# A token mixer and its MLP on one core: a written order for the opening, two attention pieces per chunk, and 512-token blocks in the second row

## The chip, the cores and the metric

The kernel runs on one core of one Trainium2 chip. The metric is the device time in microseconds (us), as the median of several runs. The core's engines work side by side, each through its own list of instructions in order, and wait for one another by semaphores: TensorE (PE in the profile; its weight loads are PEld), VectorE (DVE), ScalarE (ACT), GpSimd (POOL) and SyncE (SP, which here only issues transfers). Within the core TensorE multiplies from SBUF into eight banks of PSUM.

## The reference

Two parts. The first is a linear attention with a decay per channel, over 4 sequences (B) of 768 tokens, 8 heads of 48 channels; the second is a gated MLP over its 3072 output rows.

```python
for t in range(S):                       # S = 768
    cur = einsum('bhd,bhe->bhde', u[None] * kt, vt)
    y[:, :, t] = einsum('bhd,bhde->bhe', rt, state + cur)
    state = wt[:, :, :, None] * state + einsum('bhd,bhe->bhde', kt, vt)

x = y.transpose(0, 2, 1, 3).reshape(B * S, H * D)      # 3072 x 384
gate = 1.0 / (1.0 + exp(-(x @ w_gate)))                # 384 x 1536
val = x @ w_val
out = (gate * val) @ w_out                             # 1536 x 384
```

All of it is float32. Each MLP product is made of three products of a rounded high part (`hi`) and the rest (`lo`), in the type fp32r: lo times hi, hi times lo, hi times hi.

## The kernel before, in words

**Chunks and rows.** A sequence is cut into 6 chunks of 128 tokens. The four chunks with the same place in the four sequences make a *row*: n = 0 to 5, 512 tokens each. Chunk q is sequence q % 4 of row q // 4, and there are 24. Attention turns a chunk into 128 rows of x, and the MLP works on a row, or on half of one, in 12 slices f of 128 hidden units.

**The opening** is rows 0 and 1 (chunks 0 to 7 enter the MLP, chunks 8 to 11 are prepared). In it the 12 weight slices also come from memory for the first time and are unpacked, each by five instructions on VectorE and ScalarE. After it (row 2 on) a fixed loop takes over: a row of 512 tokens and one slice after another, with the attention of the next row's chunks spread among them, and a second look at the weights for bounds. That loop is not touched.

**Pieces.** The opening is built of small named pieces; the names below are used in the prediction, with a number for the chunk q or the slice f.

- For a chunk: `pin`, `tok` (loads on SP), `b1_` `b2_` `b4_` (three products on GpSimd), `b3_` (a sum on VectorE), `pk` and `pr` (a scan and a product each, on VectorE, lines 370 to 392), `guard` (ScalarE, line 397), `fade` (VectorE), `tk` (transposes on TensorE), `kT` (copy on ScalarE), `sm` (sums: 32 small matmuls, line 466), `mid` and `keep` (the state at mid-chunk and at the end), `sc` (scores: 32 matmuls of line 419 and 16 or 32 of line 429), `m0` `m1` (masks on VectorE, line 451), `mx` (mix: 64 small matmuls, line 490), `y0` `y1` (VectorE, line 497), `tx` (transposes of the result), `xh` and `xl` (high part on ScalarE, rest on VectorE, line 515).
- For a slice of weights: `words` (load, line 274), `wg` (ScalarE, line 281), `wb` and `wt` (VectorE, lines 286 and 290), `wh` (ScalarE, line 313), `wl` (VectorE, line 316).
- For an MLP block of group g and slice f: `pg` and `pu` (nine matmuls each, line 523), `sg` (sigmoid, ScalarE), `hm` (product, VectorE, line 541), `hh` (ScalarE, line 545), `hl` (VectorE, line 549), `dn` (down product, line 558: three matmuls of 384 columns per chunk).

**Groups.** Before, a group is two chunks, so 256 tokens: rows 0 and 1 have two groups each, and every `pg` and `pu` of the opening has 256 columns. From row 2 on they have 512, and the down product is turned (line 576).

**What sets the order.** `Plan` is a planner that runs while the program is built: each piece has an engine, a cost, what it comes after, a rank, and the buffers it takes and gives. `TURNS` ranks chunks and weight slices against each other, `COMES` orders the loads, `LAGS` ranks the groups, `ROOM` counts buffers. The planner emits a piece when its engine would be free, which gives every engine its list.

**Buffers.** Two each of `pin`, `tok`, `bon` and x; a load into one waits until its last reader is done. PSUM has one bank for `pg`, one for `pu`, four for the down sums and two for all attention pieces (`att_bank`). In the opening `sg`, `hh` and `hl` come from a pool named `early` with four buffers each; it is closed for a pool named `late` with two when the opening ends.

Of the kernel before, what the change touches and what calls it, by code (L numbers as in the profile page):

```python
# [169 lines left out]


class Plan:


    def __init__(self, room):
        self.ops, self.room = {}, dict(room)

    def add(self, name, engine, cost, after, rank, work=None, take=(), give=()):
        self.ops[name] = (engine, cost, [a for a in after if a], rank, work, take, give)

    def run(self):
        left = {n: set(o[2]) for n, o in self.ops.items()}
        room, free, ends, order, started = self.room, {}, [(0.0, "")], [], set()
        transfers = [n for n in sorted(self.ops, key=lambda n: self.ops[n][3]) if self.ops[n][0] == "SP"]
        while ends:
            now = min(ends)[0]
            for e in [e for e in ends if e[0] <= now]:
                ends.remove(e)
                if e[1] in self.ops:
                    for r in self.ops[e[1]][6]:  # L190
                        room[r] += 1
                    for n in left:
                        left[n].discard(e[1])
            moved = True
            while moved:
                moved = False
                for n in sorted((n for n in self.ops if n not in started and not left[n]), key=lambda n: self.ops[n][3]):
                    engine, cost, _, _, work, take, _ = self.ops[n]
                    if engine and free.get(engine, 0.0) > now or engine == "SP" and n != transfers[0]:
                        continue  # L200
                    if any(room[r] < take.count(r) for r in take):
                        continue
                    for r in take:
                        room[r] -= 1
                    if engine:
                        free[engine] = now + cost
                        ends.append((now + cost, "-" + n))
                    if engine == "SP":
                        transfers.pop(0)
                    ends.append((now + cost + (2.0 if engine == "SP" else 0.13 if engine else 0.0), n))  # L210
                    started.add(n)
                    order.append(n)
                    if work:
                        work()
                    moved = True
                    break
        assert len(started) == len(self.ops), sorted(set(self.ops) - started)
        return order
# [3 lines left out]
def tile_kernel(ctx: ExitStack, tc: tile.TileContext, dec: bass.AP, tok: bass.AP, wts: bass.AP, u: bass.AP, out: bass.AP):  # L222
# [388 lines left out]

    plan = Plan(ROOM)
    rank = {n: i for i, n in enumerate(TURNS.split())}
    comes = {n: i for i, n in enumerate(COMES.split())}

    def add(name, engine, cost, after, rank, f=None, *args, take=(), give=()):
        plan.add(name, engine, cost, after, rank, f and (lambda: f(*args)), take, give)

    add("ub", "SP", 1.4, [], comes["ub"], lambda: nc.sync.dma_start(ub, u.partition_broadcast(P)))
    for q in range(3 * B + 2):  # L620
        k = rank.get(f"c{q}", 99)
        add(f"pin{q}", "SP", 2.9, [], comes[f"p{q}"], load_pin, q, take=["pin"])
        add(f"tok{q}", "SP", 2.3 + 1.4 * (not q), [], comes[f"t{q}"], load_tok, q, take=["tok"])
        if q > 3 * B:
            continue
        add(f"b1_{q}", "POOL", 1.35, [f"tok{q}", "ub"], k, bonus1, q, take=["bon"])
        add(f"b2_{q}", "POOL", 1.15, [f"b1_{q}"], k, bonus2, q)
        add(f"b3_{q}", "DVE", 0.57, [f"b2_{q}"], k + 0.3, bonus3, q)
        add(f"b4_{q}", "POOL", 1.45, [f"b3_{q}"], k, bonus4, q)
        add(f"pk{q}", "DVE", 2.2, [f"pin{q}"], k, prep_k, q, take=["eg"])  # L630
        old = q >= B
        if old:
            add(f"fade{q}", "DVE", 0.38, [f"pk{q}", f"keep{q - B}"], k + 0.05, fade, q, take=["ready"])
        add(f"pr{q}", "DVE", 2.15, [f"pk{q}"], k + 0.1, prep_r, q)
        add(f"guard{q}", "ACT", 1.26, [f"pr{q}", old and f"fade{q}"], k + 0.5, guard, q, give=["eg"])
        if q == 3 * B:
            continue
        add(f"tk{q}", "PE", 0.4 + 0.5 * (q < 3), [f"pk{q}"], k + 0.1, turn_k, q, take=["bank", "kT"])
        add(f"kT{q}", "ACT", 0.52, [f"tk{q}"], k + 0.1, take_k, q, give=["bank"])
        add(f"sm{q}", "PE", 0.7 + 0.5 * (q < 3), [f"kT{q}", f"tok{q}"], k + 0.15, sums, q, take=["bank", "bank"], give=["kT"])  # L640
        add(f"mid{q}", "DVE" if old else "ACT", 0.36, [f"sm{q}", old and f"fade{q}"], k + 0.12, middle, q, take=["mid"], give=["bank"])
        add(f"keep{q}", "DVE", 0.36, [f"mid{q}"], k + 0.15, keep, q, give=["bank"])
        add(f"sc{q}", "PE", 1.2 + 1.2 * (q < 3), [f"pr{q}", f"mid{q}"], k + 0.2, scores, q, take=["bank", "bank", "at"], give=["pin"] + ["ready"] * old)
        add(f"m0{q}", "DVE", 0.43, [f"sc{q}"], k + 0.2, mask, q, 0)
        add(f"m1{q}", "DVE", 0.43, [f"m0{q}"], k + 0.2, mask, q, 1)
        add(f"mx{q}", "PE", 0.92 + 0.7 * (q < 3), [f"m1{q}"], k + 0.3, mix, q, give=["at"])
        add(f"mid{q}done", None, 0, [f"sc{q}", f"keep{q}"], k, give=["mid"])
        add(f"y0{q}", "DVE", 0.37, [f"mx{q}", f"b4_{q}"], k + 0.3, take_y, q, 0, give=["bank"])
        add(f"y1{q}", "DVE", 0.37, [f"y0{q}"], k + 0.3, take_y, q, 1, give=["bank"])
        first = q % B == 0  # L650
        add(f"tx{q}", "PE", 0.34 + 0.45 * (q < 3), [f"y1{q}", q % B and f"tx{q - 1}"], k + 0.4, turn_x, q, take=["bank"] + ["x"] * first, give=["bon"])
        add(f"xh{q}", "ACT", 0.68, [f"tx{q}"], k, take_x, q)
        add(f"xl{q}", "DVE", 0.58, [f"xh{q}"], k, rest_x, q, give=["bank"])
        add(f"tok{q}done", None, 0, [f"mx{q}", f"sm{q}", f"b4_{q}", q % B and f"tok{q - 1}done"], k, give=["tok"])
    for f in range(NFF):
        k = rank[f"w{f}"]
        add(f"words{f}", "SP", 3.7 + 1.6 * (not f), [], comes[f"w{f}"], fetch, f)
        add(f"wg{f}", "ACT", 1.29, [f"words{f}"], k, w_top, f)
        add(f"wb{f}", "DVE", 0.85, [f"words{f}", f and f"wb{f - 1}"], k, w_body, f, take=["full"])
        add(f"wt{f}", "DVE", 1.39, [f"wb{f}", f"wg{f}"], k, w_join, f)  # L660
        add(f"wh{f}", "ACT", 1.15, [f"wt{f}"], k, w_hi, f)
        add(f"wl{f}", "DVE", 1.42, [f"wh{f}"], k, w_lo, f, give=["full"])
    for g, (n, i0, i1) in enumerate(GROUPS):
        m = i1 - i0
        for f in range(NFF):
            a, name = (n, f, i0, i1), f"{g}_{f}"
            k = 100 + f + LAGS[g]
            soon = k / 1000 - 1
            up_cost = 9 * (0.008 + 0.056 * m)
            need = [f"xl{n * B + i}" for i in range(i0, i1)] + [f"wl{f}", f and f"pu{g}_{f - 1}"]  # L670
            add("pg" + name, "PE", up_cost, need, k, gate, *a, take=["pg", "unit"] + [f"po{i}" for i in range(i0, i1) if f == 0])
            add("sg" + name, "ACT", 0.14 + 0.13 * m, ["pg" + name], soon, sigmoid, *a, give=["pg"])
# [107 lines left out]
```

## Time and profile before

| | |
|---|---|
| time, median of 3 runs | 582.59 us (581.71 to 583.43) |
| the profiled execution, its own time | 581.37 us |
| its span, first to last instruction | 579.6 us |
| PE busy | 551.4 us (95%), 6330 matmuls |
| PEld busy | 476.2 us (82%) |
| DVE busy | 322.8 us (56%) |
| ACT busy | 248.3 us (43%) |
| POOL busy | 100.4 us (17%) |
| granted TensorE clock | 0.999 |

A busy time is the sum over one engine's instructions in the one profiled execution; a share is of the span. In rows of instruction groups the columns are line, engine, operation, what is written and read with its shape, and the count, then busy us and the mean ns of one, then the idle time just before them and what ended it. In rows of the timeline and the chain the first number is the start and the second the duration, in us. In rows of stretches the columns are the stretch, its length, then busy us (and count) of PE, PEld, DVE, ACT and POOL, the granted clock, the DMA share and GB/s. A wait reads "engine, line <- who ended it: us in total, times, longest".

### The profile page before, as it was taken

The page shows a single profiled execution, that of the slowest core. Times are in us where ns is not written, and L with a number is a line of the kernel's source. Part 1 is how long each engine was busy: PE and PEld are TensorE (multiplying, and loading weights), DVE is VectorE, ACT ScalarE, POOL GpSimd, SP SyncE. Part 2 cuts the span into 40 slices and gives each one's busy share as a digit, 9 for nine tenths or more (in the row PEclk, how much of TensorE's full clock was granted, in tenths as well). Part 3 has the DMA queues.
Part 4 walks back from the last instruction along what each step waited for, and adds up shares of the span by engine and source line. Part 5 has one row for each costly group of instructions (what it writes and reads, how often), then busy time and mean ns, then how long its engine had stood idle before and what let it go on. Part 6 is the DMA issues. An engine that isn't in the chain of part 4 may idle for free.

```text
span 579.6 us, 14499 instructions
## 1 busy us (share of the span) xinstructions
PE 551.4 (95%) x6330; PEld 476.2 (82%) x6330; DVE 322.8 (56%) x561; ACT 248.3 (43%) x577; POOL 100.4 (17%) x86
## 2 busy tenths in 40 slices
...
GB/s 283 181 379 366 91 365 2 44 150 95 60 98 58 138 125 1 84 151 119 88 151 101 160 151 77 131 151 55 173 185 34 173 42 43 63 19 1 1 0 58
DMA packets 17203, 67.32 MB, mean 116 GB/s; under 512 B 1904, under 2 KB 3312, under 8 KB 15600
## 3 DMA queue, kind: packets, MB, share of 16 engines
...
q8 instruction: 51, 0.84, 0.6%
q14 instruction: 16, 0.13, 0.1%
...
## 4 chain that ended last, share of the span: by engine, by line
PE 90%; DVE 6%; ACT 1%; DMA 1%; issue 1%; ACTq 0%; SPq 0%; DVEq 0%
PE pu L523 26%; PE pg L523 26%; PE po L576 17%; PE po L558 8%; PE pa L490 3%; PE pa L419 2%; PE pa L429 2%; PE pk L402 2%; PE pv L466 1%; PE px L502 1%; DMA tok<-tok 1%; PE pa L466 1%; DVE w L316 1%; DVE full L290 1%; DVE eg L370 1%
## 5 line engine op out<-in xcount | busy, mean ns | idle before, releaser
L523 PE MATMUL pg<-x,w 128*128 128x256 f32 (+1 forms) x864 | 168.0, 339 | 2.1 <-ACT sg L534 1.5
L523 PE MATMUL pu<-x,w 128*128 128x256 f32 (+1 forms) x864 | 169.8, 341 | 0.0
L523 PEld LDWEIGHTS pg<-x,w 128*128 128x128 f32 x864 | 137.3, 190 | 20.3 <-ACT sg L534 1.9
L523 PEld LDWEIGHTS pu<-x,w 128*128 128x128 f32 x864 | 135.2, 189 | 16.9
L541 DVE TENSOR_TENSOR sg<-pu,sg 128x256 f32<-128x256 f32 (+1 forms) x96 | 53.4, 556 | 120.4 <-PE pu L523 117.7
L545 ACT CAST hh<-sg 128x256 fp32r<-128x256 f32 (+1 forms) x96 | 49.2, 513 | 158.5 <-DVE sg L541 157.9
L534 ACT ACTIVATE sg<-pg 128x256 f32<-128x256 f32 (+1 forms) x96 | 47.0, 489 | 107.1 <-PE pg L523 101.3
L576 PE MATMUL po<-hh,w 128*128 128x512 f32 x288 | 89.2, 391 | 0.0
L363 POOL TENSOR_TENSOR bon<-tok,a 128x384 f32<-128x384 f32 x24 | 37.7, 1573 | 262.4 <-DVE a L359 262.4
L549 DVE TENSOR_TENSOR hl<-sg,hh 128x256 fp32r<-128x256 f32 (+1 forms) x96 | 56.9, 592 | 40.8 <-ACT hh L545 40.6
L576 PEld LDWEIGHTS po<-hh,w 128*128 128x128 f32 x288 | 54.0, 188 | 10.9
L576 PE MATMUL po<-hl,w 128*128 128x512 f32 x144 | 58.3, 405 | 0.0
L352 POOL TENSOR_TENSOR bon<-tok,ub 128x384 f32<-128x384 f32 x24 | 30.9, 1289 | 113.0 <-PE px L502 60.5
L558 PE MATMUL po<-w,hh 128*128 128x384 f32 x192 | 49.0, 336 | 0.0
L497 DVE TENSOR_TENSOR bon<-pa,bon 128x192 f32<-128x192 f32 x48 | 15.2, 351 | 46.8 <-PE pa L490 46.8
L558 PEld LDWEIGHTS po<-w,hh 128*128 128x128 f32 x192 | 34.9, 189 | 0.0
L558 PE MATMUL po<-w,hl 128*128 128x384 f32 x96 | 33.9, 353 | 0.6 <-DVE hl L549 0.6
L370 DVE TENSOR_TENSOR_SCAN eg<-pin,ends 112x516 f32<-112x516 f32 x24 | 30.2, 1257 | 4.1 <-DMA pin<-dec 4.1
L576 PEld LDWEIGHTS po<-hl,w 128*128 128x128 f32 x144 | 27.0, 188 | 5.6 <-DVE hl L549 0.2
L397 ACT ACTIVATE junk<-eg 112x1032 bf16<-112x1032 f32 x24 | 25.6, 1065 | 11.8 <-DVE eg L387 11.8
L387 DVE TENSOR_TENSOR_SCAN eg<-pin,heads 112x516 f32<-112x516 f32 x24 | 30.2, 1256 | 0.0
L355 POOL TENSOR_TENSOR bon<-bon,tok 128x384 f32<-128x384 f32 x24 | 29.6, 1233 | 1.8
...
## 6 DMA issues: line engine op xcount, KB each, us to landing
pin<-dec SPq DMA_DIRECT2D x23, 772.0 KB, 4.7
tok<-tok SPq DMA_DIRECT2D x24, 576.0 KB, 5.5
...
wraw<-wts SPq DMA_DIRECT2D x12, 1151.6 KB, 10.1
...
y<-o ACTq DMA_DIRECT2D x8, 192.0 KB, 1.9
...
```

The costliest lines, as they stand in the source:

```text
L352: nc.gpsimd.tensor_tensor(out=bon[q], in0=tk[q][:, 0:DM], in1=ub, op=ALU.mult)
L355: nc.gpsimd.tensor_tensor(out=bon[q], in0=bon[q], in1=tk[q][:, DM:2 * DM], op=ALU.mult)
L363: nc.gpsimd.tensor_tensor(out=by_head(bon[q]), in0=by_head(tk[q][:, 2 * DM:]), in1=a0, op=ALU.mult)
L370: nc.vector.tensor_tensor_scan(out=e[:, 516:0:-1], data0=t[:, 516:0:-1], data1=ends[:, 516:0:-1], initial=0.0, op0=ALU.mult, op1=ALU.add,)
L387: nc.vector.tensor_tensor_scan(out=e[:, WW:WW + 516], data0=t[:, 0:516], data1=heads[:, 0:516], initial=0.0, op0=ALU.mult, op1=ALU.add,)
L523: nc.tensor.matmul(t, lhsT=w[f][:, cols], rhs=x[n][:, a, k, i0 * C:i1 * C], start=k == 0 and j == 0, stop=k == NKT - 1 and j == 2)
L534: nc.scalar.activation(sg, hid["g", n, f, i0], AF.Sigmoid)
L541: nc.vector.tensor_tensor(out=sg, in0=hid["u", n, f, i0], in1=sg, op=ALU.mult)
L545: nc.scalar.copy(hh, hid["s", n, f, i0])
L549: nc.vector.tensor_tensor(out=hl, in0=hid["s", n, f, i0], in1=hid["hi", n, f, i0].bitcast(F32), op=ALU.subtract)
L558: nc.tensor.matmul(po[n, i][:, :DM], lhsT=h[:, c], rhs=w[f][:, 2 * DM:], start=f == 0 and j == 0, stop=f == NFF - 1 and j == 2,)
L576: nc.tensor.matmul(po[n, k], lhsT=w[f][:, cols], rhs=h, start=f == 0 and j == 0, stop=f == NFF - 1 and j == 2)
```

## The change

Three things, all in the opening.

1. The planner goes. Its place takes a string, `ORDER`, that names every piece in the order in which it is emitted; a table, `todo`, maps each name to its function.
2. `sm`, `sc` and `mx` become two pieces: `ss` (scores_sums: the 32 matmuls of line 419 and the sums, which now write to the free columns of the same two banks) and `sx` (state_mix: the matmuls of line 429 and the mix). Both functions were there already for the loop from row 2 on.
3. Row 1 becomes one group of four chunks, 512 tokens: group 2 is (1, 0, 4), and group 3 is gone. The pools change from `early` to `late` at its first piece, `pg2_0`.

The order itself changes with this. Some differences: on SP `words0` comes ahead of `tok0`, and `tok2` ahead of `tok1`; on ScalarE `wg0` comes first of all; on VectorE the unpacking of slice 0 follows `pr0` at once; the first block, `pg0_0`, comes after `tk2`, before any scores of chunk 2; and row 1 starts when row 0 is through.

```diff
-TURNS = "w10 c0 w6 c2 w1 c3 w0 c8 w3 c4 c1 c9 w7 c11 c7 w2 c6 w8 w11 w4 w5 c5 c12 c10 w9"
-COMES = "p0 t0 p1 ub w0 p2 t1 w1 t2 p3 w2 w3 w6 t3 w5 w4 w11 p4 t4 p5 w9 p6 t7 w7 t5 w10 w8 t6 t8 p7 p11 p8 t9 t11 p12 p9 p10 t10 t12 p13 t13"
-GROUPS = [(0, 0, 2), (0, 2, 4), (1, 0, 2), (1, 2, 4)]
-LAGS = [96.5, 328.5, 417.5, 78.5]
-ROOM = dict(pin=2, tok=2, bon=2, eg=1, ready=2, mid=2, kT=1, at=1, bank=2, x=2, full=1, pg=1, pu=1, unit=4, po0=1, po1=1, po2=1, po3=1)
+GROUPS = [(0, 0, 2), (0, 2, 4), (1, 0, 4)]
+ORDER = """
+pin0 words0 pk0 ub pr0 tk0 tok0 wg0 wb0 kT0 wt0 guard0 wh0 words1 wl0 b1_0 ss0 pin1 b2_0 b3_0 mid0 m00 b4_0 tok2 wg1 keep0 m10 wb1
+sx0 wt1 words2 pk1 wh1 tok1 wl1 pr1 words3 wg2 wb2 y00 b1_1 y10 pin2 tx0 wt2 tk1 xh0 kT1 xl0 b2_1 words4 wh2 ss1 b1_2 b3_1 wl2
+mid1 guard1 b4_1 m01 m11 keep1 b2_2 wg3 sx1 wb3 pk2 pin3 y01 y11 wt3 tx1 tk2 xh1 words5 wh3 xl1 pr2 pg0_0 wg4 pu0_0 kT2 wl3 sg0_0
+tok3 guard2 ss2 hm0_0 wb4 words6 hh0_0 wt4 pg0_1 mid2 pk3 pu0_1 sg0_1 wh4 words10 pg0_2 wg5 b1_3 hm0_1 b3_2 pu0_2 m02 sg0_2 b2_3
+keep2 hh0_1 m12 pg0_3 wl4 sx2 b4_2 hm0_2 hl0_0 wb5 wt5 pu0_3 pin4 y02 wh5 y12 dn0_0 pr3 hh0_2 words7 tx2 sg0_3 pg0_4 xh2 hm0_3
+hl0_1 hh0_3 pu0_4 wl5 guard3 tk3 sg0_4 tok6 xl2 dn0_1 kT3 hm0_4 wg6 hl0_2 ss3 hl0_3 pk4 hh0_4 dn0_2 mid3 pg0_5 wb6 wt6 dn0_3 b3_3
+wh6 pu0_5 keep3 b4_3 m03 m13 wg7 wl6 sx3 sg0_5 hl0_4 pg0_6 hm0_5 tok4 wb7 hh0_5 wg10 y03 pu0_6 y13 fade4 words8 hl0_5 pr4 tx3
+dn0_4 xh3 sg0_6 dn0_5 xl3 b1_4 pin5 tk4 pg1_0 wt7 kT4 ss4 b2_4 hm0_6 wh7 words9 pu1_0 mid4 b1_6 hh0_6 m04 sg1_0 b3_4 wg8 pg1_1
...
+pu0_11 sg0_11 dn1_9 b4_11 hm0_11 m011 pg1_11 hh0_11 hl1_10 b1_8 mid11 keep11 pu1_11 sg1_11 m111 guard8 hl0_11 sx11 b2_8 dn0_11
+y011 pin12 hm1_11 hh1_11 dn1_10 hl1_11 y111 tk8 dn1_11 kT8 ss8 m08 pg2_0 mid8 m18 b3_8 keep8 b4_8 pu2_0 sg2_0 pg2_1 hm2_0 hh2_0
+hl2_0 pu2_1 pk12 sg2_1 dn2_0 hm2_1 hh2_1 hl2_1 sx8 pr12 pg2_2 tok9 y08 y18 fade12 pin9 dn2_1 sg2_2 guard12 tx8 pu2_2 xh8 b1_9 b2_9
...
+hh2_9 guard10 hl2_9 tx10 pg2_10 b1_12 b2_12 dn2_9 sg2_10 xh10 pu2_10 pg2_11 hm2_10 hh2_10 hl2_10 pu2_11 sg2_11 dn2_10 hm2_11
+hh2_11 hl2_11 tx11 xl10 dn2_11 xh11 xl11 b3_12 b4_12 ahead
+"""
...
-class Plan:
...
-    def scores(q):
-        pairs(q)
-        from_state(q)
...
-    def sums(q):
-        for s in range(2):
-            bank["v", q, s] = att_bank(f"pv{q}_{s}")[:L, :NP * D].rearrange("a (p e) -> a p e", e=D)
-        add_up(q)
...
-    plan.run()
-    early.__exit__(None, None, None)
-    stage = own.enter_context(tc.tile_pool(name="late", bufs=2))
+    for kind in ORDER.split():
+        if kind == "pg2_0":
+            early.__exit__(None, None, None)
+            stage = own.enter_context(tc.tile_pool(name="late", bufs=2))
+        todo[kind]()
     late = True
```

The pieces that took their place, there before and after:

```python
def scores_sums(q):
    pairs(q)
    for s in range(2):
        bank["v", q, s] = bank["y", q, s][:L]
    add_up(q)

def state_mix(q):
    from_state(q)
    mix(q)
```

More of the change, by code (lines that the diff above doesn't have):

```diff
@@ L1 @@
-import heapq
 from contextlib import ExitStack
@@ new lines @@
+keep4 b4_4 hm1_0 m14 guard4 wl7 pu1_1 words11 sg1_1 sx4 hl0_6 wb8 wt8 pg0_7 tok5 hm1_1 dn0_6 pk5 hh1_1 sg0_7 hh1_0 pin6 wh8 pu0_7
+hl1_0 pg1_2 y04 hm0_7 pr5 dn1_0 sg1_2 wg9 pu1_2 hl1_1 hh0_7 wl8 pg1_3 dn1_1 fade5 sg1_3 hm1_2 guard5 y14 wb9 tk5 pu1_3 hl0_7 kT5
+pk6 tx4 dn0_7 xh4 hh1_2 pg0_8 xl4 b1_5 hm1_3 ss5 wt9 sg0_8 pg1_4 mid5 b2_6 m05 pu0_8 hl1_2 sg1_4 b2_5 b3_6 wg11 keep5 m15 dn1_2
+b4_6 b3_5 hm0_8 sx5 b4_5 hh0_8 hh1_3 wh9 pr6 pu1_4 pin7 pg1_5 hl0_8 hl1_3 hm1_4 tok7 dn1_3 y05 hh1_4 y15 sg1_5 wl9 pu1_5 wb10
@@ new lines @@
+dn0_8 hl1_4 wt10 tx5 tk6 xh5 pg0_9 kT6 b1_7 hm1_5 wh10 xl5 dn1_4 fade6 b2_7 guard6 ss6 wl10 sg0_9 hh1_5 pu0_9 mid6 hl1_5 pg0_10
+m06 m16 hm0_9 dn1_5 sg0_10 hh0_9 hl0_9 pu0_10 keep6 pk7 pg1_6 sx6 sg1_6 wb11 hm0_10 pu1_6 y06 tok11 y16 tx6 hm1_6 dn0_9 pin11
+fade7 hh1_6 b3_7 xh6 hl1_6 tk7 pr7 pg1_7 kT7 pu1_7 sg1_7 xl6 b1_11 pg1_8 wt11 ss7 sg1_8 b4_7 dn1_6 m07 hm1_7 b2_11 mid7 hh1_7 m17
+pu1_8 guard7 keep7 hl1_7 sx7 pk11 pg1_9 pin8 y07 hm1_8 pr11 dn1_7 sg1_9 hh0_10 wh11 tok8 pu1_9 hh1_8 y17 fade11 tk11 hm1_9 pg1_10
@@ new lines @@
+kT11 hl1_8 wl11 hh1_9 tx7 pu1_10 xh7 sg1_10 xl7 guard11 dn1_8 hl0_10 pk8 ss11 dn0_10 hm1_10 hl1_9 hh1_10 pg0_11 fade8 b3_11 pr8
+pu0_11 sg0_11 dn1_9 b4_11 hm0_11 m011 pg1_11 hh0_11 hl1_10 b1_8 mid11 keep11 pu1_11 sg1_11 m111 guard8 hl0_11 sx11 b2_8 dn0_11
+y011 pin12 hm1_11 hh1_11 dn1_10 hl1_11 y111 tk8 dn1_11 kT8 ss8 m08 pg2_0 mid8 m18 b3_8 keep8 b4_8 pu2_0 sg2_0 pg2_1 hm2_0 hh2_0
+hl2_0 pu2_1 pk12 sg2_1 dn2_0 hm2_1 hh2_1 hl2_1 sx8 pr12 pg2_2 tok9 y08 y18 fade12 pin9 dn2_1 sg2_2 guard12 tx8 pu2_2 xh8 b1_9 b2_9
@@ new lines @@
+pg2_3 hm2_2 pk9 hh2_2 pu2_3 sg2_3 hl2_2 fade9 pr9 dn2_2 hm2_3 tk9 pg2_4 kT9 hh2_3 guard9 hl2_3 xl8 pu2_4 sg2_4 b3_9 b4_9 dn2_3
+hm2_4 hh2_4 ss9 pg2_5 mid9 keep9 m09 m19 sx9 sg2_5 pu2_5 y09 pin10 y19 hl2_4 dn2_4 tok10 hm2_5 hh2_5 hl2_5 tx9 pk10 pg2_6 b1_10
+dn2_5 sg2_6 xh9 pr10 pu2_6 b2_10 tk10 hm2_6 pg2_7 kT10 xl9 hh2_6 fade10 hl2_6 b3_10 pu2_7 sg2_7 b4_10 dn2_6 ss10 pg2_8 mid10 m010
+keep10 hm2_7 m110 hh2_7 pu2_8 sg2_8 hl2_7 dn2_7 hm2_8 hh2_8 sx10 pg2_9 y010 tok13 y110 hl2_8 tok12 pu2_9 sg2_9 pin13 dn2_8 hm2_9
@@ L169, in general @@
             nc.sync.dma_start(to, x.rearrange("p (k c) -> p k c", c=C))
-class Plan:
[L175 to L218, printed above, removed]
 @with_exitstack
@@ L609, in add_bounds @@
         nc.vector.tensor_scalar(out=flag, in0=total[:1, :1], scalar1=float(P * 5 * SEEN), scalar2=None, op0=ALU.not_equal)
[L612 to L619, printed above, removed]
@@ L620, in tile_kernel @@
-    for q in range(3 * B + 2):
[L621 to L654, printed above, removed]
@@ L655, in tile_kernel @@
-    for f in range(NFF):
[L656 to L672, printed above, removed]
-            add("pu" + name, "PE", up_cost, ["pg" + name], k, value, *a, take=["pu"])
-            add("hm" + name, "DVE", 0.15 + 0.135 * m, ["pu" + name, "sg" + name], soon, hidden, *a, give=["pu"])
-            add("hh" + name, "ACT", 0.14 + 0.13 * m, ["hm" + name], soon, hidden_hi, *a)
-            add("hl" + name, "DVE", 0.15 + 0.14 * m, ["hh" + name], soon, hidden_lo, *a)
-            ends_here = f == NFF - 1
-            add("dn" + name, "PE", 0.52 * m, ["hl" + name, f and f"dn{g}_{f - 1}"], k - 0.5, down, *a, give=["unit"])
-            if ends_here:
-                add("out" + name, "ACT", 0.5 * m, ["dn" + name], soon, give=[f"po{i}" for i in range(i0, i1)])
@@ L681, in tile_kernel @@
-    ahead = (2, 0, 0, B)
-    add("ahead", "PE", 2.1, [f"xl{2 * B + i}" for i in range(B)] + ["pg2_11", "pg3_11"], 200, gate, *ahead, take=["pg"])
-    for n in range(2):
-        add(f"x{n}done", None, 0, [f"pu{g}_{NFF - 1}" for g in range(len(GROUPS)) if GROUPS[g][0] == n], 0, give=["x"])
-    plan.run()
-    early.__exit__(None, None, None)
-    stage = own.enter_context(tc.tile_pool(name="late", bufs=2))
+    ahead = (2, 0, 0, B)
+    todo = {"ub": lambda: nc.sync.dma_start(ub, u.partition_broadcast(P)), "ahead": lambda: gate(*ahead)}
@@ new lines, in name @@
+    def name(kind, f, *a):
+        todo[kind] = lambda: f(*a)
+    for q in range(3 * B + 2):
+        for kind, f in (
+            ("pin", load_pin), ("tok", load_tok), ("b1_", bonus1), ("b2_", bonus2), ("b3_", bonus3), ("b4_", bonus4),
+            ("pk", prep_k), ("fade", fade), ("pr", prep_r), ("guard", guard), ("tk", turn_k), ("kT", take_k), ("ss", scores_sums),
+            ("mid", middle), ("keep", keep), ("sx", state_mix), ("tx", turn_x), ("xh", take_x), ("xl", rest_x),
+        ):
+            name(f"{kind}{q}", f, q)
+        for o in range(2):
+            name(f"m{o}{q}", mask, q, o)
+            name(f"y{o}{q}", take_y, q, o)
```

6 lines of the change are left out of this document (added).

## The prediction

> **What bounds the kernel now.** I began with the page and its chain of waits.
>
> ```profile
> span 579.6 us, 14499 instructions
> ...
> PE 90%; DVE 6%; ACT 1%; DMA 1%; issue 1%; ACTq 0%; SPq 0%; DVEq 0%
> ```
>
> TensorE carries the end of the kernel. As an average that says little about the opening, the only part that changes, so next I read busy time by stretches (columns: stretch, length, then busy us of PE, PEld, DVE, ACT, POOL).
>
> ```profile
> 0.00:40.00 40.00, 20.49 (x391) 16.25 (x391) 33.18 (x44) 16.04 (x26) 14.78 (x23) 1.00 0.72 269
> 40.00:60.00 20.00, 18.75 (x312) 17.53 (x311) 17.12 (x28) 14.25 (x22) 6.45 (x5) 1.00 0.94 368
> 60.00:237.00 177.00, 174.92 (x2407) 167.65 (x2406) 122.58 (x229) 66.87 (x148) 36.30 (x27) 1.00 0.27 99
> 237.00:579.60 342.60, 337.26 (x3228) 274.81 (x3226) 149.96 (x262) 151.10 (x382) 42.88 (x31) 1.00 0.27 92
> ```
>
> Until 40 us VectorE is the busy engine (33.2 of 40). From 40 to 237, where row 2 takes over, TensorE idles only 1.25 + 2.08 = 3.3 us. What follows 237 has the same code before and after, and I count it as unchanged. So the opening's end is: when TensorE gets its first MLP block, plus its work after that, plus its idle time. I price these three. The timeline of TensorE shows the first:
>
> ```profile
> 39.02 1.04 PE L429 MATMUL pa<-mid,pin 48*64 48x48 f32 x16
> 39.99 2.29 PE L523 MATMUL pg<-x,w 128*128 128x256 f32 x9
> 42.07 1.37 PE L523 MATMUL pu<-x,w 128*128 128x256 f32 x9
> ```
>
> **Step 1, blocks of 512.** Row 1 has 12 slices times two sides; each was two runs of nine matmuls of 256 columns and becomes one run of nine of 512. Their prices are the distances between starts: in the timeline (first fence, the last three lines are blocks back to back) and in the chain (second fence).
>
> ```profile
> 48.61 1.23 PE L523 MATMUL pg<-x,w 128*128 128x256 f32 x9
> 49.78 0.68 PE L466 MATMUL pv<-tok,kT 64*64 64x48 f32 x32
> 50.38 1.34 PE L523 MATMUL pu<-x,w 128*128 128x256 f32 x9
> ...
> 94.13 1.23 PE L523 MATMUL pg<-x,w 128*128 128x256 f32 x9
> 95.20 1.24 PE L523 MATMUL pu<-x,w 128*128 128x256 f32 x9
> 96.28 1.24 PE L523 MATMUL pg<-x,w 128*128 128x256 f32 x9
> ```
>
> ```profile
> 251.00 2.04 PE pu L523 x9
> 253.04 2.04 PE po L576 x9
> ```
>
> Nine of 256 take 1.07 to 1.08 us, nine of 512 take 2.04. Each pair saves 2 x 1.075 - 2.04 = 0.11, and 24 pairs save **2.6 us**, all on the path, as TensorE has hardly any idle time there. The down products keep their count and shape. VectorE and ScalarE also get fewer, longer instructions in row 1, which costs and gains nothing there: VectorE has 54 us to spare in 60 to 237. The 512-wide buffers now open at pg2_0 in place of the end; their first sigmoid waits for row 0's last down product, which stands just ahead of pg2_0, and the four output copies of row 1 come together on ScalarE ahead of row 2's sigmoid. I cost both at nothing: a block of 2.04 covers each, and beyond it each us would be lost.
>
> The Trainium skill ("TensorE: Matmul & The Clock Gate", section "Back-to-back issue gap") gives a warm isolated gap of N/2.4 + 2.5 ns. By that rule, as an estimate, 256 columns cost 109 ns and 512 cost 216, and the 24 pairs would save only 0.6 us. That would put the sum below at -0.1. The trace has 119 and 227 ns, 11 ns a matmul in place of 2.5, so it does not agree, and I go by the trace.
>
> **Step 2, two attention pieces.** sums, scores and mix become scores_sums and state_mix; the instructions are the same, but one visit to small tiles falls away per chunk. At 48.61 the nine matmuls ahead of a small piece take 1.17 and not 1.07, and the nine that begin at 50.38 take 1.18 up to the next start: each visit costs about 0.1 + 0.1 = 0.2 us. Behind the first MLP block there are 28 visits now (mix of chunk 2, three for each of chunks 3 to 11) and 20 after (two for each of chunks 2 to 11): 8 x 0.2 = **1.6 us** saved. A chunk also takes two of the attention banks fewer, which costs nothing.
>
> **Step 3, the start.** VectorE releases the first block through the last subtraction of chunk 1's x (xl1); before, it ended at 38.05 (first row below). The other rows are VectorE's means over the opening:
>
> ```profile
> 37.50 0.55 DVE L515 TENSOR_TENSOR x<-px,x 128x384 fp32r<-128x384 f32 x1
> ...
> L290 DVE SCALAR_TENSOR_TENSOR full<-wraw,full 128x1152 int32<-128x1152 int32 x12 | 18.3, 1525 | 0.1
> L316 DVE TENSOR_TENSOR w<-full,w 128x1152 fp32r<-128x1152 f32 x12 | 17.1, 1427 | 1.5 <-ACT w L313 1.5
> L370 DVE TENSOR_TENSOR_SCAN eg<-pin,ends 112x516 f32<-112x516 f32 x13 | 16.7, 1286 | 4.1 <-DMA pin<-dec 4.1
> L387 DVE TENSOR_TENSOR_SCAN eg<-pin,heads 112x516 f32<-112x516 f32 x13 | 16.7, 1284 | 0.0
> L392 DVE TENSOR_TENSOR pin<-pin,eg 112x512 f32<-112x512 f32 x13 | 10.2, 786 | 0.4
> L286 DVE TENSOR_SCALAR full<-wraw 128x1152 int32<-128x1152 int32 x12 | 10.0, 837 | 0.0
> L376 DVE TENSOR_TENSOR pin<-pin,eg 112x512 f32<-112x512 f32 x13 | 9.7, 750 | 0.0
> ```
>
> Ahead of xl1 the written order has one pk (1.29 + 0.75 and a reciprocal, 2.2), two pr (1.28 + 0.79 = 2.07 each) and a small b3 and keep (0.9) fewer: 7.2 us less. It has two wb (0.84), two wt (1.53) and one wl (1.43) more: 6.2 us. Net -1.0.
>
> The waits go the other way. VectorE starts at 3.7 (row further down), and pk0 and pr0 take it to about 7.7. Weight slice 0 now stands right behind them, and its load is issued second, ahead of tok0. Loads land as the queue's bytes do (KB, us from issue to landing; then three issues with their times):
>
> ```profile
> tok<-tok SPq DMA_DIRECT2D x1, 576.0 KB, 5.9
> pin<-dec SPq DMA_DIRECT2D x1, 772.0 KB, 7.3
> ub<-u SPq DMA_DIRECT2D x1, 192.0 KB, 8.6
> wraw<-wts SPq DMA_DIRECT2D x1, 1151.6 KB, 10.9
> ...
> 1.82 0.43 SPq L335 DMA_DIRECT2D tok<-tok  x1
> 2.29 0.43 SPq L330 DMA_DIRECT2D pin<-dec  x1
> 3.25 0.43 SPq L274 DMA_DIRECT2D wraw<-wts  x1
> ```
>
> Counted from the first issue, 1348 KB had landed at 7.7 us (tok0), 2120 at 9.6 (pin1), 3464 at 14.2 (words0). words0 after stands at 1924 KB: **9.2 us**, with 7.7 and 14.2 as bounds. So VectorE waits 1.5. ScalarE then does top (wg0), the copy of kT0 and guard0 before wh0:
>
> ```profile
> L281 ACT ACTIVATE wraw<-wraw 128x1152 int32<-128x1152 uint8 x4 | 5.0, 1256 | 0.0
> L397 ACT ACTIVATE junk<-eg 112x1032 bf16<-112x1032 f32 x4 | 4.2, 1062 | 4.5 <-DVE eg L387 4.5
> L313 ACT CAST w<-full 128x1152 fp32r<-128x1152 f32 x2 | 2.3, 1152 | 2.3 <-DVE full L290 2.3
> L406 ACT COPY kT<-pk 128x448 f32<-128x448 f32 x4 | 2.1, 533 | 8.7 <-PE pk L402 8.6
> ```
>
> wg0 ends at 10.5 (wt0 waits 0.5), kT0 at 11.0, guard0 at 12.3, wh0 at 13.4, where wt0 was done at 11.9: wl0 waits 1.5. Later wl2 and xl0 wait about 1.5 together, behind wh2 and kT1 and behind the turn of x. Waits after: 5.0.
>
> ```profile
> DVE eg L370 <- DMA pin<-dec: 3.7, 1, 3.7
> ...
> 0.00:38.05 38.05, 18.59 (x344) 14.44 (x344) 31.33 (x43) 14.09 (x23) 14.78 (x23) 1.00 0.71 262
> ```
>
> Waits before: 38.05 - 31.33 - 3.7 = 3.0. So xl1 ends at 38.05 - 1.0 + 2.0 = 39.1; the first block follows at once, at 39.2, where before two other pieces held it to 40.0: **-0.8 us**. Against that, TensorE has done less attention by then: chunk 2's sums (0.60 at 49.78, or 19 ns for each of 32 small matmuls), its 48 matmuls of scores (0.9 at that rate) and chunk 3's turn (some 0.2): **+1.7**.
>
> tok1 is loaded third among the tok loads, when tok0's buffer is free, so SP holds words3, pin2 and words4 behind state_mix of chunk 0. That ends near 18.5; tok1 then lands near 24, and b3_1 asks for its product near 28, so I cost it nothing. If that cover goes, each us late is a us at the start.
>
> **Step 4, idle time after the start.** The order works up seven weight slices where now six are used twice over. Walking the written order by these durations, TensorE waits: pu0_2 for hm0_1, 0.3; tx2 for y12 behind wb5 and wt5, 0.75; pg0_4 for sg0_3, which stands on ScalarE behind wh5, 1.2; sx3 for its second mask behind pk4, wb6, wt6, 1.1; pg1_0 for xl3 behind pr4, 0.55. That is 3.9; later pieces have slack, and I add 0.6: 4.5 against 3.3, **+1.2 us**. Bounds: 1 and 8.5 (rivals 3 and 2).
>
> **The sum:** -2.6 - 1.6 - 0.8 + 1.7 + 1.2 = -2.1 us. The profiled execution took 581.37 (span 579.6), so 579.3. It lies 1.2 under the runs' median, 582.59, which would give 580.5. I take **579.8**.
>
> **Rivals.** *1, slower: slice 0 lands late.* If words0 shares the queue with all that is issued behind it and lands at 14.2, as it does now, the start moves by 5.0 and the sum is +2.9: 584.3 to 585.5. It decides from a landing at 11.3. For it: its own row. Against: pin1, with words0 behind it, landed by its place in the queue. *2, VectorE starves TensorE.* An instruction that meets GpSimd is stretched:
>
> ```profile
> 76.67 2.12 DVE L290 SCALAR_TENSOR_TENSOR full<-wraw,full 128x1152 int32<-128x1152 int32 x1
> ...
> 86.94 1.35 DVE L290 SCALAR_TENSOR_TENSOR full<-wraw,full 128x1152 int32<-128x1152 int32 x1
> ```
>
> That is 0.8 over the second row. Five GpSimd products stand between pg0_0 and pg1_0; if each costs that on the path, idle time is 8.5 and the sum +1.9: 583.3 to 584.5. The Trainium skill ("SBUF — State Buffer", section "SBUF: two separate sides") has VectorE and GpSimd lock a shared port for a whole instruction; the trace agrees, at 2.12 against 1.35. *3, faster: the waits of step 4 vanish* because VectorE runs ahead, idle time 1: sum -5.6, 575.8 to 577.0. For it: before, VectorE fed TensorE with 1.25 idle in 40 to 60. *4, the wide blocks bring nothing:* with one bank each for pg and pu, TensorE waits in row 1 for the longer sigmoids and products as long as it saves. Sum +0.5: 581.9 to 583.1. Against: at 251.00 blocks of 512 follow each other without a gap, with the same banks.
>
> **Chances.** Forecast 0.42, rival 1 0.13, rival 2 0.20, rival 3 0.20, rival 4 0.05. About 0.3% (1.75 us) is what a measurement can tell. Faster means under 580.8, so the forecast is faster in 0.30 of its 0.42 and same in 0.12; rival 2 is slower in 0.10, and same in 0.10 where fewer of the five lie on the path. Faster 0.50, same 0.27, slower 0.23. The range runs from rival 3, with 1 us for a start at the early bound of the landing, to rival 1: 574.5 to 585.5; the forecast's own is 578 to 582.
>
> **What would show it.** Groups by shape: 216 matmuls each of 256 columns for pg and pu, 432 + 216 of 512. Start of the first pg near 39.2 (step 3), wb0 near 9.2. TensorE idle between it and row 2 near 4.5, under tx2, pg0_4, sx3. Row 2's first pu near 235 in place of 237. A first block after 42, or idle time above 7, makes the prediction wrong.

## The result and the profile after

The change made the kernel slower: 590.06 us (median of 4 runs, 589.54 to 591.75) against 582.19 (4 runs, 581.71 to 583.43), a ratio of 1.0144 with a 95% interval of 1.013 to 1.0158. The profiled execution took 591.75, with a span of 590.0 and a granted clock of 0.988 (before: 0.999). In the kernel after, the lines are others: blocks (`pg`, `pu`) 487, sigmoid 498, `hm` 505, `hl` 513, down product 522, output copy 528 and its store 529, `kT` 380, `xh` 475.

The page of the kernel after: its head, the granted clock in tenths over 40 slices of 14.75 us, and the chain of waits by engine.

```profile
span 590.0 us, 13998 instructions
...
PEclk9999999999799999799999999999999999999999
...
PE 88%; DVE 3%; DMA 3%; ACT 2%; issue 1%; POOL 1%; SPq 0%; ACTq 0%; DVEq 0%; POOLq 0%
```

Two slices have a 7 where before there was none, the 11th (147.5 to 162) and the 17th (236 to 251). The chain has gained DMA and ScalarE. Busy time by stretches (columns as before) finds the same two places:

```profile
40.00:60.00 20.00, 17.07 (x308) 15.74 (x308) 19.17 (x31) 12.24 (x24) 4.25 (x3) 1.00 0.66 262
...
140.00:150.00 10.00, 4.70 (x67) 3.98 (x54) 1.38 (x4) 2.62 (x6) 0.00 (x0) 0.95 0.62 199
150.00:160.00 10.00, 9.71 (x89) 8.09 (x90) 2.71 (x7) 1.45 (x3) 0.83 (x1) 0.71 0.05 20
...
240.00:250.00 10.00, 8.21 (x58) 6.29 (x62) 1.39 (x3) 2.19 (x5) 2.79 (x3) 0.66 0.12 41
```

From 140 to 150 TensorE works 4.70 of 10 us, and then it is "busy" at a clock of 0.71. The waits of TensorE from 40 to 240, and then of the rest:

```profile
PE pa L393 <- ACT kT L380: 4.8, 1, 4.8
PE pu L487 <- DVE sg L505: 2.2, 1, 2.2
PE po L522 <- DVE hl L513: 0.8, 1, 0.8
PE pg L487 <- ACT sg L498: 0.7, 1, 0.7
...
PE pg L487 <- ACT x L475: 3.4, 1, 3.4
```

The two long ones wait for ScalarE, which is 41% busy. The timeline says what stands ahead of these pieces there. First at 141 to 156, where row 0 ends:

```profile
142.14 0.48 ACT L528 COPY o<-po 128x384 f32<-128x384 f32 x1 [0.46 <-PE po L522]
...
147.87 0.48 ACT L528 COPY o<-po 128x384 f32<-128x384 f32 x1 [4.43 <-DMA y<-o]
...
149.70 0.53 ACT L380 COPY kT<-pk 128x448 f32<-128x448 f32 x1 [0.41 <-ACT o L528]
150.29 1.02 PE L393 MATMUL pa<-pin 48*64 48x64 f32 x27 [4.76 <-ACT kT L380]
...
152.16 4.00 PE L487 MATMUL pg<-x,w 128*128 128x512 f32 x9
156.00 2.25 PE L487 MATMUL pu<-x,w 128*128 128x512 f32 x9
```

**Stall A.** The last down product of a row (`dn0_11`, `dn1_11`) also emits the copies of its sums to an output buffer and their stores. Both groups of row 0 end here, so four copies meet. There are two output buffers; the third copy waits 4.43 us for the store of the first. `kT8`, which chunk 8's `ss8` needs, stands behind them on ScalarE. When it comes, TensorE is slow: the first block takes 3.84 us (152.16 to 156.00) where the next takes 2.08. The cost: 4.8 and 0.8 idle, 1.8 in the block, and 0.8 in `ss8` (150.29 to 152.16, where it takes 1.07 in the kernel both_first below), 8.2 us in all. The idle 0.8 is a wait for `hl1_11`, whose `hh1_11` stands behind the first two copies alone; both_first has it too.

```profile
236.87 0.48 ACT L528 COPY o<-po 128x384 f32<-128x384 f32 x1 [1.60 <-PE po L522]
...
239.31 0.48 ACT L528 COPY o<-po 128x384 f32<-128x384 f32 x1 [1.08 <-DMA y<-o]
...
241.15 0.49 ACT L475 ACTIVATE x<-px 128x384 fp32r<-128x384 f32 x1 [0.41 <-ACT o L528]
...
241.79 4.38 PE L487 MATMUL pg<-x,w 128*128 128x512 f32 x9 [3.37 <-ACT x L475]
245.96 0.95 PE L376 MATMUL pk<-ident,pin 112*128 112x112 f32 x4
246.59 2.93 PE L487 MATMUL pu<-x,w 128*128 128x512 f32 x9
```

**Stall B.** Row 1 ends as one group, with four copies at once. `xh11`, the high part of chunk 11's x, is emitted behind `dn2_11` and so stands behind them; without it row 2's first block (`ahead`) can't start. Cost: 3.37 idle; then a block of 4.17 (241.79 to 245.96) in place of 2.04, and 1.1 more in the next two pieces, 6.6 us in all. Before, the groups ended one by one, with two copies each: row 0's 12 us apart (first copies at 130.79 and 142.80), row 1's 3.6 (232.78 and 236.36). No copy waited for a store then; the first ones of the second groups in the kernel before:

```profile
142.80 0.48 ACT L564 COPY o<-po 128x384 f32<-128x384 f32 x1 [1.21 <-PE po L558]
...
236.36 0.48 ACT L564 COPY o<-po 128x384 f32<-128x384 f32 x1 [1.34 <-PE po L558]
```

The store that the third copy waits for took 5.8 us in the first place and 1.9 in the second (transfers of the two stretches: KB, us from issue to landing):

```profile
y<-o ACTq DMA_DIRECT2D x2, 192.0 KB, 5.8
```

```profile
y<-o ACTq DMA_DIRECT2D x4, 192.0 KB, 1.9
```

In the first stretch loads of 772 and 576 KB were on their way; that these are the cause was not tested. Without both stalls the span would be 590.0 - 14.8 = 575.2, or 576.0 if the wait of 0.8 stays.

### The profile page after: what moved, and what is told of

The parts are those of the page before. It is cut to its first block, busy times and chain, and to the rows that moved or that the text cites. A ratio compares the mean times of both kernels' runs of the same rounds, so it can differ in the third digit from the quotient of the medians.

```text
span 590.0 us, 13998 instructions
## 1 busy us (share of the span) xinstructions
PE 550.6 (93%) x6114; PEld 467.4 (79%) x6114; DVE 313.9 (53%) x537; ACT 243.0 (41%) x553; POOL 96.3 (16%) x86
## 4 chain that ended last, share of the span: by engine, by line
PE 88%; DVE 3%; DMA 3%; ACT 2%; issue 1%; POOL 1%; SPq 0%; ACTq 0%; DVEq 0%; POOLq 0%
PE pg L487 26%; PE pu L487 25%; PE po L540 17%; PE po L522 8%; PE pa L454 3%; PE pa L403 2%; PE pa L393 2%; PE pa L430 2%; DMA tok<-tok 2%; PE pk L376 1%; PE px L466 1%; DMA y<-o 1%; ACT w L287 1%; DVE eg L344 1%; ACT o L528 0%
## 5 line engine op out<-in xcount | busy, mean ns | idle before, releaser
L487 PE MATMUL pg<-x,w 128*128 128x512 f32 (+1 forms) x756 | 169.6, 370 | 4.1 <-ACT x L475 3.4
L487 PE MATMUL pu<-x,w 128*128 128x512 f32 (+1 forms) x756 | 166.9, 365 | 2.2 <-DVE sg L505 2.2
L487 PEld LDWEIGHTS pg<-x,w 128*128 128x128 f32 x756 | 131.3, 193 | 27.5 <-ACT x L475 4.0
L487 PEld LDWEIGHTS pu<-x,w 128*128 128x128 f32 x756 | 128.0, 190 | 23.4 <-DVE sg L505 2.4
L505 DVE TENSOR_TENSOR sg<-pu,sg 128x512 f32<-128x512 f32 (+1 forms) x84 | 51.4, 612 | 124.2 <-PE pu L487 122.9
L509 ACT CAST hh<-sg 128x512 fp32r<-128x512 f32 (+1 forms) x84 | 46.8, 558 | 161.6 <-DVE sg L505 161.2
L498 ACT ACTIVATE sg<-pg 128x512 f32<-128x512 f32 (+1 forms) x84 | 44.8, 533 | 106.8 <-PE pg L487 105.7
L337 POOL TENSOR_TENSOR bon<-tok,a 128x384 f32<-128x384 f32 x24 | 31.3, 1304 | 277.7 <-DVE a L333 277.7
L513 DVE TENSOR_TENSOR hl<-sg,hh 128x512 fp32r<-128x512 f32 (+1 forms) x84 | 51.7, 618 | 42.3 <-ACT hh L509 42.3
L393 PEld LDWEIGHTS pa<-pin 48*64 48x64 f32 x768 | 15.3, 144 | 16.4 <-ACT kT L380 8.0
## 6 DMA issues: line engine op xcount, KB each, us to landing
tok<-tok SPq DMA_DIRECT2D x24, 576.0 KB, 5.8
```

Of the source, the lines that this page charges most:

```text
L337: nc.gpsimd.tensor_tensor(out=by_head(bon[q]), in0=by_head(tk[q][:, 2 * DM:]), in1=a0, op=ALU.mult)
L487: nc.tensor.matmul(t, lhsT=w[f][:, cols], rhs=x[n][:, a, k, i0 * C:i1 * C], start=k == 0 and j == 0, stop=k == NKT - 1 and j == 2)
L498: nc.scalar.activation(sg, hid["g", n, f, i0], AF.Sigmoid)
L505: nc.vector.tensor_tensor(out=sg, in0=hid["u", n, f, i0], in1=sg, op=ALU.mult)
L509: nc.scalar.copy(hh, hid["s", n, f, i0])
L513: nc.vector.tensor_tensor(out=hl, in0=hid["s", n, f, i0], in1=hid["hi", n, f, i0].bitcast(F32), op=ALU.subtract)
```

## The experiments

Before is timed again beside each: 581.78 us for the first four, 581.96 for the next four, 581.63 for the last two. The intervals are of the ratio to before. The kernel after was timed beside the 582.19 alone; with each run set against its own before, the differences between kernels named below come out 0.2 to 0.4 us smaller.

**kt_first and xh_first: each gating piece alone put ahead of the copies.** Only the place in the written order changes.

```diff
 # kt_first
-tk8 dn1_11 kT8 ss8
+tk8 kT8 dn1_11 ss8
 # xh_first
-tx11 xl10 dn2_11 xh11 xl11 b3_12
+tx11 xl10 xh11 xl11 dn2_11 b3_12
```

> One swap in the changed kernel's order: kT8 is emitted ahead of dn1_11, so on ScalarE the copy that scores_sums of chunk 8 waits for stands ahead of the second pair of row 0's output copies. Position theory: the idle 4.8 us at 145 goes, and with it the slow matmuls behind it (pg2_0 took 3.84 in place of 2.04, the small matmuls 1.0 more): 590.1 - 7.6 = 582.5. Rival, the written order loses its time elsewhere and this stall is only where it shows: another wait takes its place within a few us, 588 to 590. Rival, only the idle time counts and the clock does not: 585.3.

> One other swap: xh11 and xl11 are emitted ahead of dn2_11, so ScalarE makes the last part of row 2's x before the four output copies of row 1. Position theory: the 3.4 us of idle time at 238 goes, and the slow blocks behind it (pg 4.2 and pu 2.9 in place of 2.04 each, the turn 0.3 more): 590.1 - 6.7 = 583.4. Without the clock's part: 586.7. If row 2's first sigmoid, which now stands behind the four copies, is late in its turn: 586 or more.

Measured: kt_first 583.74 us, ratio 1.003 [1.002, 1.0039]; xh_first 584.58, 1.0047 [1.0029, 1.0066]. So stall A cost 590.06 - 583.74 = 6.3 and stall B 5.5. In each trace its own wait is gone and the other's is there, at 4.8 and 3.4 as in the kernel after. Both came some 1.2 us above the expectation, which took costs read in the profiled execution, the slowest of its four at 591.75, off the median of 590.06.

**both_first: the two swaps together.**

> Both swaps. Position theory: the two gains add, 590.1 - 14.3 = 575.8, that is 6 us under the kernel before. Rival (the order starves TensorE in row 0 anyway): not under 582.

Measured: 577.43 us, 0.9919 [0.99, 0.9939], 12.6 below the kernel after, where the two alone gave 6.3 + 5.5 = 11.8. It beats the kernel before by 4.35 us. The timeline where row 0 ends:

```profile
144.13 0.53 ACT L380 COPY kT<-pk 128x448 f32<-128x448 f32 x1
...
145.97 0.69 PE L393 MATMUL pa<-pin 48*64 48x64 f32 x32
...
147.04 2.37 PE L487 MATMUL pg<-x,w 128*128 128x512 f32 x9
148.51 0.48 ACT L528 COPY o<-po 128x384 f32<-128x384 f32 x1 [3.86 <-DMA y<-o]
149.24 2.21 PE L487 MATMUL pu<-x,w 128*128 128x512 f32 x9
```

The third copy still waits 3.86 us for its buffer, and nobody waits for it. The copies' work and the stores are as long as ever; only what stood behind them has moved.

**four_o: the order of the kernel after, with an output buffer for each chunk.** It tells the place from the buffers.

```diff
-                o = p2.tile([P, DM], F32, tag="o", name=f"o{n}_{i}")
+                o = p1.tile([P, DM], F32, tag=("ot0", "ot1", "ot2", "o")[i], name=f"o{n}_{i}")
```

> The changed kernel's order as it is, but the output tiles of the opening have a buffer for each of the four chunks (three of them the tiles that later rows use, so no more memory) in place of two in turn. If the copies' wait for the landing of the first two outputs makes the stalls, both go and the time is near 576, as with both swaps. If their place ahead of kT8 and xh11 is enough, four copies at 0.95 us each stay: the stall at 145 shrinks from 4.8 to 1.7 and its slow matmuls go (5.9 us), the one at 238 shrinks by 0.7, or by 4.0 if the clock then holds: 580 to 583.5.

Measured: 586.1 us, 1.0054 [1.0029, 1.0079], short of both theories. The five times are not alike: three are 586.1 to 586.6, at a granted clock of 0.990 or 0.991, and two 583.7 and 583.9, at 0.995. The trace is of one of the three. No copy waits for a store now, but the waits stay in part, and so does the slow block after them:

```profile
147.07 1.02 PE L393 MATMUL pa<-pin 48*64 48x64 f32 x27 [1.61 <-ACT kT L380]
...
148.94 4.16 PE L487 MATMUL pg<-x,w 128*128 128x512 f32 x9
152.93 2.21 PE L487 MATMUL pu<-x,w 128*128 128x512 f32 x9
```

TensorE idled 1.61 us and then took 3.99 for a block (148.94 to 152.93). So in the median a buffer each is worth 4.0 of the 12.6, about what the waits lost (4.8 - 1.6 and 3.4 - 2.8); an idle stretch a third as long still brought a slow block here. The two faster times would fit one slow block fewer, which no trace shows. In the best of the five the buffers gain 6.4, so the place on ScalarE counts for more.

**warm: the kernel after, with TensorE kept busy through both stalls.** 20 and 14 matmuls of 512 columns, whose result nobody reads, go into the bank of `pg` ahead of `ss8` and of `ahead`.

```diff
+    def keep_warm(count):
+        t = ps1.tile([P, 512], F32, tag="pg", name=f"warm{count}")
+        for i in range(count):
+            nc.tensor.matmul(t, lhsT=whi[0][:, :P], rhs=x[1][:, 0, 0], start=True, stop=True)
-tk8 dn1_11 kT8 ss8
+tk8 dn1_11 kT8 warm20 ss8
-b3_12 b4_12 ahead
+b3_12 b4_12 warm14 ahead
```

> The changed kernel in its own order, with matmuls that nobody reads put into the two stalls: 20 of 512 columns (4.5 us) ahead of scores_sums of chunk 8, 14 (3.2 us) ahead of row 2's first block. They fit into the idle time, so nothing starts later. If TensorE's slow pace behind the stalls comes of the idle time itself, it goes: pg2_0 and row 2's first pg and pu take 2.04 each again, 590.1 - 6.1 = 584.0. If the slow pace has another cause (the loads in flight, the switch of buffers), the time stays at 590.

Measured: 586.55 us, 1.0076 [1.006, 1.0091], so 3.5 below the kernel after. The stall itself is as before (`ss8` starts at 150.07), but the blocks behind it run at full pace:

```profile
149.93 0.53 ACT L380 COPY kT<-pk 128x448 f32<-128x448 f32 x1 [0.41 <-ACT o L528]
150.07 1.07 PE L393 MATMUL pa<-pin 48*64 48x64 f32 x29
...
151.57 2.33 PE L487 MATMUL pg<-x,w 128*128 128x512 f32 x9
153.74 2.20 PE L487 MATMUL pu<-x,w 128*128 128x512 f32 x9
```

2.17 for the block in place of 3.84; behind the second stall it is 2.54 (239.54 to 242.08) in place of 4.17. Slow blocks thus come from the idle time ahead of them, and not from what else runs then. The gain was some 2.5 us under the expectation; part of that is a wait at 45 us which was 2.7 in this run (2.2 in the kernel after) and had a slow clock behind it. In the profiled executions the spans differ by more, 590.0 - 584.9 = 5.1, as the one of the kernel after lies 1.7 above its median. What else is in it stays open.

**halves: both_first, with row 1's blocks in two halves of 256 columns again, in the same bank.**

```diff
+        step = 2 if n == 1 else i1 - i0
+        for i in range(i0, i1, step):
...
-                    t, lhsT=w[f][:, cols], rhs=x[n][:, a, k, i0 * C:i1 * C], start=k == 0 and j == 0, stop=k == NKT - 1 and j == 2)
+                        t[:, (i - i0) * C:(i - i0 + step) * C], lhsT=w[f][:, cols], rhs=x[n][:, a, k, i * C:(i + step) * C],
+                        start=k == 0 and j == 0, stop=k == NKT - 1 and j == 2)
```

> The order with both swaps (577.4), and the blocks of row 1 worked in two halves of 256 columns into the same bank, all else as it was: undoes the wide blocks alone. By the measured distances (1.075 for nine of 256, 2.04 for nine of 512): 24 x 0.11 = 2.6 us more, 580.0. By the rule of the Trainium skill (an estimate from its page on TensorE and the clock gate) 0.6 more, 578.0. If row 1 is bound by something else: 577.4.

Measured: 579.11 us, 0.9949 [0.9936, 0.9963]: 1.7 above both_first. A pair of halves back to back:

```profile
165.69 2.32 PE L489 MATMUL pg<-x,w 128*128 128x256 f32 x18
167.85 2.32 PE L489 MATMUL pu<-x,w 128*128 128x256 f32 x18
```

From start to start 2.16 us for 18 matmuls, 0.12 more than 9 of 512. That is the price of the prediction, but over 24 blocks it would give 2.9; 1.7 was measured. By the two traces it lies between: from `ss8` to row 2's first block, with no idle time in either, TensorE takes 87.53 us here and 85.48 in both_first, 2.05 more.

**visits: both_first, with the mix of chunks 4 to 11 a visit of its own again,** one MLP piece behind the state's products (chunk 4 as the example).

```diff
-sx4 hl0_6 wb8 wt8 pg0_7 tok5
+fs4 hl0_6 wb8 wt8 pg0_7 mx4 tok5
...
-            ("sx", state_mix),
+            ("sx", state_mix), ("fs", from_state), ("mx", mix),
```

> The order with both swaps (577.4), with state_mix of chunks 4 to 11 split again into its two halves and one block or down product of the MLP between them: three visits to small tiles per chunk in place of two. At 0.2 us a visit, 8 visits: 1.6 more, 579.0. If a visit costs nothing beside its own matmuls: 577.4. If the mix coming a block later delays VectorE and the chain behind it: over 580.

Measured: 581.55 us, 0.9996 [0.9987, 1.0005]: 4.1 above both_first. TensorE from 36 to 260, first both_first and then visits:

```profile
36.00:260.00 224.00, 221.20 (x2913) 199.86 (x2912) 152.87 (x265) 92.57 (x192) 43.52 (x36) 0.99 0.34 125
```

```profile
36.00:260.00 224.00, 218.60 (x2885) 195.40 (x2886) 148.30 (x259) 89.96 (x184) 41.27 (x36) 1.00 0.33 123
```

TensorE idles 5.4 us in place of 2.8: what waits for the mix comes a block later. That leaves 4.1 - 2.6 = 1.5 us for eight visits, or 0.2 each. In the profiled execution the first block came 1 us earlier than in both_first (36.10 against 37.13) and no slow blocks followed at 48, so there they may cost up to 0.3 each.

**words0_later: both_first, with the load of slice 0 issued behind tok0.**

```diff
-pin0 words0 pk0 ub pr0 tk0 tok0 wg0 wb0
+pin0 pk0 ub pr0 tk0 tok0 words0 wg0 wb0
```

> The order with both swaps (577.4), and the load of weight slice 0 moved behind tok0 on SP, nothing else. By the bytes ahead of it, it lands near 12.3 in place of 9.4, and VectorE and ScalarE, which have slice 0 right behind pr0, wait for it: the first block starts up to 2.9 later, 580.3. If the earlier tok0 pays that back (b3_0 waits 0.9 for GpSimd now, the scores of chunk 0 wait for kT0): 578 to 579. If the start is not bound by this load: 577.4.

Measured: 579.65 us, 0.9958 [0.9944, 0.9971]: 2.2 above both_first. VectorE gets the slice at 12.50 where it was 9.39 in the kernel after:

```profile
12.50 0.76 DVE L260 TENSOR_SCALAR full<-wraw 128x1152 int32<-128x1152 int32 x1 [4.39 <-DMA wraw<-wts]
...
38.84 2.67 PE L487 MATMUL pg<-x,w 128*128 128x256 f32 x9
```

3.1 us later there and 1.7 to 2.1 later at the first block (37.13 in both_first, 36.77 in the kernel after): the opening gives back a third.

**pk_later and best: the waits that both_first still has.** pk_later moves chunk 3's first scan behind `hm0_1`; best also puts `hm1_11` and `hh1_11` ahead of row 0's last down products.

```diff
 # pk_later and best
-mid2 pk3 pu0_1 sg0_1 wh4 words10 pg0_2 wg5 b1_3 hm0_1 b3_2
+mid2 pu0_1 sg0_1 wh4 words10 pg0_2 wg5 b1_3 hm0_1 pk3 b3_2
 # best alone
-sx11 b2_8 dn0_11 y011 pin12 hm1_11 hh1_11 dn1_10
+sx11 b2_8 y011 hm1_11 hh1_11 dn0_11 pin12 dn1_10
```

> Both gating pieces stay ahead of the output copies (577.43), and pk3 (a scan, reciprocals and a product, 2.04 + 0.18 + 0.66 = 2.9 us of VectorE) goes behind hm0_1 instead of ahead of it. Theory: the wait of pu0_2 for hm0_1 (1.96 at 47.90) goes, and with it the slow clock of 47 to 51 that follows it (blocks of 2.1 and 1.7 in place of 1.24, some 1.3): 574.1 to 575.5. Rival: VectorE is behind there in any order (3.0 us of other work come either way before b3_3 and pk3's heirs), so the wait turns up a little later at another piece, with a cooled clock again: 577 or more.

> As the one before, and besides hm1_11 and hh1_11 stand ahead of row 0's last turned-down block, so that hh1_11 no longer stands behind that block's two output copies on ScalarE. Theory: the wait of 0.8 of row 0's last block for hl1_11 goes too, some 0.8 below the kernel with pk3 alone: 573.3 to 574.7. Rival: row 0's last block then waits for its own copies or for TensorE's longer queue, and the time stays within 0.3 of the kernel with pk3 alone.

Measured: 577.52 us, 0.9927 [0.9913, 0.9941], and 577.04, 0.992 [0.9906, 0.9934]. Neither can be told from both_first's 0.9919 [0.99, 0.9939]. The waits of TensorE from 38 to 260, first in both_first and then in pk_later:

```profile
PE pu L487 <- DVE sg L505: 2.0, 1, 2.0
PE po L522 <- DVE hl L513: 0.8, 1, 0.8
```

```profile
PE pg L487 <- ACT sg L498: 1.7, 2, 1.0
PE po L522 <- DVE hl L513: 0.8, 1, 0.8
PE px L466 <- DVE bon L461: 0.5, 1, 0.5
```

The wait of 2.0 for `hm0_1` turned into three of 2.2 together, as the rival had it: VectorE is behind there in any order (18.99 of 20 us busy from 40 to 60 in both_first). best took the 0.8 away too, but its waits for sigmoids are 2.3 where pk_later's are 1.7; what is left is less than can be told. The gain over before stands at 0.8%.

## Why the prediction was wrong

The forecast was 579.8 and the result 590.06, outside the range and on the other side. What the change was costed for did come about; the miss is two stalls that it had at nothing.

**The step that failed** is the last part of step 1, "the four output copies of row 1 come together on ScalarE ahead of row 2's sigmoid. I cost both at nothing: a block of 2.04 covers each". The copies were seen and the wrong follower named. Ahead of the sigmoid stands `xh11`, without which there is no block to cover anything; and four copies with their waits take from 236.87 to 241.15, 4.3 us and not 2. Stall A was missed outright: the walk through the order took a down product as a TensorE piece, and did not see that at the last slice it also puts copies on ScalarE's list, nor that both groups of row 0 end together ahead of `kT8`. The words "later pieces have slack, and I add 0.6" of step 4 failed with it. The words "beyond it each us would be lost" was too mild as well: an idle us could cost more than itself, where the next block ran at half pace. The prediction's own sign, idle time above 7, did come: 11.9 us from 36 to 260. No rival had this mechanism; those that ended slower were put at the start and on VectorE.

**Step 1, wide blocks:** forecast -2.6, measured -1.7 (halves). The shapes are as foretold, 216 matmuls of 256 columns for each of `pg` and `pu`; of 512 each has 432 + 108 (216 is both together). The Trainium skill ("TensorE: Matmul & The Clock Gate", section "Back-to-back issue gap") would give, as an estimate by its constant of 2.5 ns a matmul, 24 x 9 x 2.5 ns = 0.5 (the prediction has 0.6). The trace disagrees: 1.7 was measured. The back-to-back price (0.12 a block) is further above, so the step was right in sign and half as large again as what came.

**Step 2, visits:** forecast -1.6 at 0.2 each; the experiment puts the visit at 0.2 to 0.3, and shows besides 2.6 us more of idle time when the mix is split.

**Step 3, the start:** mis-sized. The landing was right (9.2 forecast, 9.39 measured; words0_later confirms that it counts), rival 1 did not come true, and the waits were near (5.0 forecast; 6.0 measured, 37.32 less the first wait of 3.7 and less 27.64 of work). But the first block started at 36.77 and not 39.2, so this term is -3.2 in place of -0.8. It starts before `xl1` ends, at 37.32, as its first matmul reads only the high part, and then waits; by the start of the second block (39.24 against 42.07) the term is -2.8. The timeline, and VectorE's work up to the end of `xl1`:

```profile
9.39 0.76 DVE L260 TENSOR_SCALAR full<-wraw 128x1152 int32<-128x1152 int32 x1 [1.69 <-DMA wraw<-wts]
...
36.76 0.56 DVE L479 TENSOR_TENSOR x<-px,x 128x384 fp32r<-128x384 f32 x1 [0.40 <-ACT x L475]
36.77 2.67 PE L487 MATMUL pg<-x,w 128*128 128x256 f32 x9
39.24 1.46 PE L487 MATMUL pu<-x,w 128*128 128x256 f32 x9
```

```profile
0.00:37.32 37.32, 15.36 (x307) 12.64 (x307) 27.64 (x39) 15.02 (x21) 14.25 (x22) 1.00 0.83 307
```

27.64 us where the means of the whole opening gave 30.3. Of the seven operations priced, `wb`, both scans and the products run below those means here (751 ns in place of 837, 1.22 us in place of 1.28), and the `pr` were long before: four took 9.7 us (one of them 2.02 + 1.30), the two left take 3.8, so 5.8 went where 4.1 was deducted. Less attention done by then (+1.7) was not tested by itself.

**Step 4, idle time:** near in size if the stalls are set aside, wrong in place. Without the two long waits 3.7 us are idle from 36 to 260, and in both_first 2.8, where 4.5 was forecast. pu0_2 waits 2.2 us and not 0.3, for `hm0_1` behind `wt4` and a scan. These took 2.06 and 2.04 while GpSimd was busy, where `wt5` and the next scan take 1.36 and 1.23: some 1.5 us, which is rival 2's mechanism at one place. pg0_4 waits 0.7 for its sigmoid where 1.2 was forecast; tx2, sx3 and pg1_0 do not wait at all.

**The sum without the stalls** is that of both_first: -4.35 us in the medians. The terms, measured but for the second, which is the forecast's: first block -2.9 (37.13 against 39.99), less attention +1.7, wide blocks -1.7, visits -1.6 to -2.6, idle time -0.5 (2.8 against 3.3), and some +1.5 for two blocks at a slow clock at 48: -3.5 to -4.5. The 577.43 lies below the forecast's own 578 to 582 and 0.4 above rival 3's 575.8 to 577.0. That nearness is luck and not rival 3's mechanism: a wait of 2.0 for VectorE is still there, and the largest term that gained is the early first block. Row 2's first `pu` starts at 233.85 in both_first (235 forecast) and at 246.59 in the kernel after.
